# Score tiles of two key tiles, earlier transposes, and three loads in new places, in an attention and spectral-mixing kernel on one Trainium2 core

## The chip, the cores and the metric

The kernel runs on one core of one Trainium2 chip. The core has five engines with queues of their own: PE (TensorE: matrix products; its weight loads are listed as PEld), DVE (VectorE), ACT (ScalarE), POOL (GpSimd) and SP (SyncE, which here only issues DMA). An engine works through its own instructions in order and waits on semaphores for the others. Sixteen DMA engines move data between the chip's memory (HBM) and the on-chip SBUF; matrix products land in PSUM, of which this kernel uses eight banks.

The metric is the device time of one execution in microseconds. Three runs of the kernel before took 470.34, 473.37 and 477.15 us; the median is 473.37.

## The reference

Two layers follow each other. Sizes: batch B = 8, heads H = 8, sequence S = 576, head size D = 64, so the model width is 512; 64 Fourier modes.

```python
# attention: causal, window of 128, a linear bias per head
scores = matmul(q, k.T) / sqrt(64)
rel = pos[:, None] - pos[None, :]
bias = -slope[h] * abs(rel)                 # slope[h] = 2 ** (-8 (h + 1) / 8)
mask = (rel >= 0) & (rel < 128)
attn = softmax(where(mask, scores + bias, -1e9))
x = matmul(attn, v)                         # heads side by side: [8, 576, 512]

# spectral mixing
X = rfft(x, axis=1)[:, :64]
Yr = einsum('bmd,mde->bme', Xr, w_r) - einsum('bmd,mde->bme', Xi, w_i)
Yi = einsum('bmd,mde->bme', Xr, w_i) + einsum('bmd,mde->bme', Xi, w_r)
u = x + irfft(Y, n=576)
out = u + maximum(u @ w_ch, 0)
```

q, k and v have 28 MB together, w_r and w_i 67 MB each, w_ch 1 MB, the output 9.4 MB, all in float32.

## The kernel before, in words

**Units and slots.** A unit is a pair of heads s of one batch b; there are 32. Units of pair 0 come first (units 0 to 7), then pairs 1, 2 and 3 batch by batch (units 8 to 31). The main loop runs slots: slot n (`_slot`) does the scores of unit n, the transposes of unit n + 1, the casts of q and k of unit n + 2 and of v of unit n + 1, the product with v (`_av`) of unit n - 1 and the Fourier transform (`_spectrum`) of unit n - 2. The order in which the functions are called is the order of the instructions on each engine: nothing is rescheduled.

**One unit.** `_load_unit` loads q and k (rows of 2304 B on 128 partitions), `_load_v` the first 512 tokens of v (rows of 512 B). POOL casts them to bfloat16 (`_cast_qk`, `_cast_v`). PE transposes q and k in 36 small products (`_tr`, two PSUM banks), ACT evacuates them (`_evac`). `_score` makes one of four key tiles: eight (four pairs for two halves) products of 64x256 for two key tiles together, an exponential on ACT of 128x512 (448 for the last tile) and a product with a mask on DVE. The mask is exp(-slope x distance), zero outside the window, so the bias and the window cost one multiplication. `_av` multiplies by v with a column of ones, which gives the sum of the softmax beside the result, and DVE divides (L495 to L501). The PSUM tile `av` exists once, so the division of unit n - 1 has to be done before PE starts `av` of unit n.

**The last 64 tokens of v** of a head pair, for all batches, are one tile `vt` (`_load_vt`): two DMAs on POOL's own queue with runs of 256 B, cast on POOL (`_cast_vt`). For pair 0 that is done in the setup, for pairs 1 to 3 in slots 2 to 4 (loads) and 4 to 6 (casts).

**Weights of the modes.** The 512 input channels are split into group 0 (pair 0's 128 channels) and group 1 (the other 384). Group 0's weights are 32 tiles, each with two modes (2 x 512 KB), group 1's 64 tiles, one mode each (2 x 768 KB). `_modes` multiplies them; group 0 within slots 10 to 35, group 1 in the late stage. A ring of three tiles (RING = 3) holds them, so tile i + 3 is sent when PE has used tile i.

**SyncE's queue.** All loads but `vt` stand in one queue in the order written: the first 16 units before the loop, with the first three weight tiles among them, then in slot n unit n + 8, v of unit n + 5, and that slot's weight tiles. q and k have 9 buffers, v has 6. The program also makes each DMA of this queue wait for the one eight before it.

**The late stage.** After the slots, group 1's 64 tiles are loaded one after the other; between them PE does the channel products x @ w_ch (`_xt`, `_xw`), which need w_ch in bfloat16 (`g.wch`), and the inverse Fourier tables (`_ft`, into `g.FT`). w_ch is loaded in two halves in slots 12 and 16 and cast on POOL in slots 14 and 18. `_finish` then puts the output together.

**PSUM.** One bank for the modes (`acc`), two for `av`, one for the Fourier products (`xt`), two for scores (`sc`, 512 columns each, also used by `_spectrum_swap`), two for transposes.

## Time and profile before

| | |
|---|---|
| median of three runs | 473.37 us (470.34 to 477.15) |
| span of the profiled execution | 471.9 us; the page gives no other time of its own |
| PE / DVE / ACT / POOL busy | 359.0 / 230.7 / 190.2 / 157.5 us |
| mean granted clock of TensorE | 0.812 |
| moved by DMA | 174.00 MB, 369 GB/s over the span |
| waits of SyncE before group 1's weights | 94.1 us on PE's modes, 83.8 us on its transposes |
| PE's idle time before mode products of group 1 | 35.4 us, for wi |

How to read it: PE is busy most of the span, but much of that is waiting inside pipelined products and a lowered clock. The DMA share says how much of the time the sixteen DMA engines had packets; it comes out a little over 1 in places. The same share goes with different rates, since short rows cost more per byte. The attention's slots lie between about 8 and 173 us, group 0's last tiles are used at 185, the late stage runs to about 430, and the end (`_finish`) to 472.

### The profile page before, as it was taken

To read this page: it belongs to the slowest core of one execution; us is meant where nothing else is said; L and a number is where in the kernel's file an instruction comes from. 1 tells how busy PE (TensorE), PEld (TensorE's weight loads), DVE (VectorE), ACT (ScalarE), POOL (GpSimd) and SP (SyncE) were. 2 spreads that over 40 slices of the span, in tenths; PEclk is the share of its full clock that TensorE was granted. 3 is DMA by queue.
4 is the path that set the end of the run, shared out by engine and by line. 5 is a ranking of instruction groups with operands and counts; after the bars stand their busy time and mean duration, and the time that the engine had idled before them with its cause. 6 is when DMAs were issued, how large, how long until landed. Compare 5 with 4: busy or idle time off the path is not lost.

```text
span 471.9 us, 15044 instructions
## 1 busy us (share of the span) xinstructions
PE 359.0 (76%) x6417; PEld 240.8 (51%) x6417; DVE 230.7 (49%) x504; ACT 190.2 (40%) x359; POOL 157.5 (33%) x264
## 2 busy tenths in 40 slices
PE   2777687977988754789787788888878798746983
PEld 2655476766776642434444444444444465424542
DVE  8677866668586551342324333333333353103884
ACT  3887676576774720123211111111122132102772
POOL 7799975786784500001000000000000000000995
PEclk9988978596797995777978878777777789555998
DMA  8999989999999999998999999999999999992677
GB/s 247 352 360 291 306 264 380 389 394 391 365 372 367 341 350 419 423 422 331 355 409 421 424 422 424 422 421 420 423 422 423 422 411 420 422 425 109 251 269 269
DMA packets 60515, 174.00 MB, mean 369 GB/s; under 512 B 5920, under 2 KB 22304, under 8 KB 60448
## 3 DMA queue, kind: packets, MB, share of 16 engines
q1 hardware_dynamic: 60064, 171.99, 94.8%
q0 software_dynamic: 384, 1.05, 1.0%
q8 instruction: 50, 0.82, 0.7%
q14 instruction: 17, 0.14, 0.1%
HBM read 163.58 MB, written 9.44 MB: 367 GB/s over the span
## 4 chain that ended last, share of the span: by engine, by line
DMA 46%; PE 32%; DVE 7%; issue 7%; ACT 4%; POOL 2%; SPq 0%; POOLq 0%; ACTq 0%; DVEq 0%
DMA wi<-in_moe_w_i_dram 46%; PE sc L436 7%; PE tqk L410 4%; PE av L489 3%; PE xt L534 3%; PE xw L761 3%; PE acc L702 3%; PE acc L733 2%; PE acc L698 2%; PE mm L761 2%; ACT qkT L418 1%; PE tp L752 1%; DVE r L890 1%; ACT att L448 1%; POOL o L898 1%
## 5 line engine op out<-in xcount | busy, mean ns | idle before, releaser
L779 ACT CAST hl<-xw 128x512 bf16<-128x512 f32 x72 | 42.1, 585 | 153.3 <-PE xw L761 153.3
L898 POOL TENSOR_TENSOR o<-r,ys 128x512 f32<-128x512 f32 x25 | 30.8, 1279 | 214.6 <-ACT ys L889 214.6
L761 PE MATMUL xw<-wch,xT 128*64 128x512 bf16 x576 | 96.0, 474 | 0.0
L780 DVE TENSOR_TENSOR hl<-xw,hl 64x512 bf16<-64x512 f32 x72 | 50.0, 695 | 81.2 <-ACT hl L779 81.2
L448 ACT ACTIVATE att<-sc 128x512 bf16<-128x512 f32 (+1 forms) x128 | 73.0, 595 | 34.4 <-PE sc L436 33.0
L702 PE MATMUL acc<-Xlast,wi 128*128 128x16 bf16 x768 | 55.3, 193 | 35.4 <-DMA wi<-in_moe_w_i_dram 35.4
L399 POOL CAST vb<-v 64x256 bf16<-64x256 f32 x128 | 65.4, 511 | 20.0 <-PE av L489 14.4
L702 PEld LDWEIGHTS <-wi 128*128 128x128 bf16 x768 | 49.1, 103 | 39.2 <-DMA wi<-in_moe_w_i_dram 39.1
L698 PE MATMUL acc<-Xlast,wr 128*128 128x16 bf16 x768 | 58.8, 193 | 13.0 <-DMA wr<-in_moe_w_r_dram 10.3
L698 PEld LDWEIGHTS <-wr 128*128 128x128 bf16 x768 | 50.2, 103 | 35.7 <-issue 21.2
L451 DVE TENSOR_TENSOR att<-att,mask 128x512 bf16<-128x512 bf16 x96 | 51.5, 559 | 30.6 <-ACT att L448 30.3
L436 PE MATMUL sc<-qkT,qkT 64*64 64x256 bf16 (+1 forms) x512 | 52.0, 313 | 18.4 <-ACT att L448 5.8
L761 PEld LDWEIGHTS <-xT 128*64 128x64 bf16 x576 | 38.5, 134 | 40.3 <-issue 24.9
L436 PEld LDWEIGHTS <-qkT 64*64 64x64 bf16 x512 | 29.1, 121 | 27.8 <-issue 18.6
L418 ACT COPY qkT<-tqk 128x576 bf16<-128x576 bf16 x64 | 41.3, 647 | 4.3 <-PE tqk L410 4.3
L410 PE MATMUL tqk<-ident_b,qkb 64*64 64x64 bf16 x1152 | 32.0, 211 | 12.5 <-issue 7.2
L754 DVE COPY xT<-tp 128x512 bf16<-128x512 bf16 x36 | 15.2, 423 | 53.5 <-PE tp L752 53.0
L410 PEld LDWEIGHTS <-qkb 64*64 64x64 bf16 x1152 | 31.7, 127 | 12.8 <-issue 6.8
L489 PE MATMUL av<-vb,att 64*128 64x65 bf16 (+1 forms) x1024 | 30.1, 204 | 3.5 <-issue 3.5
L489 PEld LDWEIGHTS <-att 64*128 64x128 bf16 (+1 forms) x1088 | 25.1, 104 | 9.9 <-issue 6.7
L388 POOL CAST qkb<-k 128x576 bf16<-128x576 f32 x32 | 26.1, 815 | 0.7 <-PE tqk L410 0.7
L388 POOL CAST qkb<-q 128x576 bf16<-128x576 f32 x32 | 22.7, 711 | 6.1 <-PE tqk L410 3.9
(124 smaller groups left out, 480.8 us busy)
## 6 DMA issues: line engine op xcount, KB each, us to landing
wr<-in_moe_w_r_dram SPq DMA_DIRECT2D x64, 768.0 KB, 8.2
wi<-in_moe_w_i_dram SPq DMA_DIRECT2D x64, 768.0 KB, 9.6
wr<-in_moe_w_r_dram SPq DMA_DIRECT2D x32, 512.0 KB, 6.5
wi<-in_moe_w_i_dram SPq DMA_DIRECT2D x32, 512.0 KB, 7.0
q<-in_q_dram SPq DMA_DIRECT2D x32, 288.0 KB, 6.7
k<-in_k_dram SPq DMA_DIRECT2D x32, 288.0 KB, 6.3
v<-in_v_dram SPq DMA_DIRECT2D x64, 128.0 KB, 6.1
out_dram<-o SPq DMA_DIRECT2D x32, 256.0 KB, 2.2
```

Source lines behind the costliest of these rows:

```text
L388: g.nc.gpsimd.tensor_copy(tb, t)
L399: g.nc.gpsimd.tensor_copy(o[64 * hh : 64 * hh + 64, i], u.v[64 * i : 64 * i + 64, hh])
L410: g.nc.tensor.transpose(tp[hs, r, :], u.b[w][hs, r], g.ident_b[hs, hs], tile_position=(64 * hh, 64 * hh))
L418: g.nc.scalar.copy(dst.rearrange("c (p r) -> c p r", r=g.R), u.tp[w].rearrange("c r p -> c p r"))
L436: nc.tensor.matmul(sc[hs, r * nq : (r + 1) * nq], lhsT=kT[hs, kt * P + r : kt * P + P : 2], rhs=qT[hs, kt * P : kt * P + nq], start=True, ...
L448: nc.scalar.activation(a[:, :cols], sc[:, :cols], AF.Exp, scale=1.0 / math.sqrt(g.D))
L451: nc.vector.tensor_tensor(out=a, in0=a, in1=g.mask[:, s], op=ALU.mult)
L489: nc.tensor.matmul(av[o, hh, col(t)], lhsT=a[hs, c0 : c0 + m], rhs=vb[hs, 0 : D + 1], start=(j == 0), stop=(j == len(terms) - 1), tile_pos ...
L698: nc.tensor.matmul(o, lhsT=wr[:, a].bitcast(BF16)[:, 1::2][:, c], rhs=X[:, a, 1:3, :, m], start=(a == 0), stop=False)
L702: nc.tensor.matmul(o, lhsT=wi[:, a].bitcast(BF16)[:, 1::2][:, c], rhs=X[:, a, 0:2, :, m], start=False, stop=(a == A - 1))
L761: nc.tensor.matmul(out[64 * h : 64 * h + 64], lhsT=lhsT[h], rhs=rhs[h], tile_position=(0, 64 * h), **kw)
L780: nc.vector.tensor_tensor(out=hl[64:128], in0=xw[64:128], in1=hl[64:128], op=ALU.subtract)
```

## The change

- `_score` makes two key tiles in one PSUM tile of two banks (`sc`, one buffer, in the pool `ps2`), with one exponential of 1024 (or 960) columns and one mask product (`_masked`), where there were four of 512 and 448. Slot n does half 0, then half 1.
- Transposes run two units ahead (`n + 2`), k before q, one after each half of the scores; casts of q and k three units ahead. Evacuated q and k have three buffers instead of two. Slot 0 does units 1 and 2.
- `_spectrum_swap` uses the bank of `xt`.
- The last tokens of v go through SyncE's queue, after the loads of units 0, 10, 11 and 13, and DVE casts them, in the same slots as before.
- w_ch is loaded in one DMA after the slots, into the last four tiles of `hl` as a buffer, behind the first three tiles of group 1; POOL casts it in one operation. `FT` and `wch` are allocated in the late stage.
- In the setup the slopes are set by POOL, the distances of the last tile share a tile with the others, the first mask is made earlier and the others after slots 1, 2 and 3.

```diff
 def _score / _masked
+    sc = g.ps2.tile([P, 1024], FP32, tag="sc", name="sc")
+    for j in range(2):
+        c = 2 * k + j
+        nq = min(256, g.S - c * P)
...
+    a = g.work.tile([P, 1024], BF16, tag=f"att{k}", name=f"att{k}")
     nc.scalar.activation(a[:, :cols], sc[:, :cols], AF.Exp, scale=1.0 / math.sqrt(g.D))
...
+def _masked(g, n, k):
+    a, m = g.unit[n].att[k], g.mask[:, g.units[n][1]]
+    if k == 0:
+        a = a.rearrange("p (j c) -> p j c", j=2)
+        m = m[:, 0:512].unsqueeze(1).broadcast_to([P, 2, 512])
+    else:
+        a = a[:, 0:960]
+    g.nc.vector.tensor_tensor(out=a, in0=a, in1=m, op=ALU.mult)

 def _slot
+    nxt = [m for m in ((1, 2) if n == 0 else (n + 2,)) if m < N]
     if n < N:
         _score(g, n, 0)
-        _score(g, n, 1)
-    if n + 1 < N:
-        _tr(g, n + 1, 0)
-        _evac(g, n + 1, 0)
-        _tr(g, n + 1, 1)
+        _masked(g, n, 0)
+    for m in nxt:
+        _tr(g, m, 1)
+        _evac(g, m, 1)
     for w in w0:
         _modes(g, *w)
     if n < N:
-        _score(g, n, 2)
-    if n + 1 < N:
-        _evac(g, n + 1, 1)
-    if n < N:
-        _score(g, n, 3)
-    if n + 2 < N:
-        _cast_qk(g, n + 2)
+        _score(g, n, 1)
+    for m in nxt:
+        _tr(g, m, 0)
+        _evac(g, m, 0)
+    if n + 3 < N:
+        _cast_qk(g, n + 3)
     if n + 1 < N:
         _cast_v(g, n + 1)
+    if n < N:
+        _masked(g, n, 1)
...
-            if n == g.first[j + 1] - 6 + i:
-                _load_vt(g, s)

 _spectrum_swap
-    sw = g.ps1.tile([P, 4, 2, g.NM], FP32, tag="sc", name="sw")
+    sw = g.ps2.tile([P, 4, 2, g.NM], FP32, tag="xt", name="sw")

 _load_vt / _cast_vt, and where the first 16 units are loaded
-        g.nc.gpsimd.dma_start(
+        g.nc.sync.dma_start(
...
-    g.nc.gpsimd.tensor_copy(g.vbt[:, s, :, 0 : g.D], g.unit.pop(("vt", s)))
+    g.nc.vector.tensor_copy(g.vbt[:, s, :, 0 : g.D], g.unit.pop(("vt", s)))
...
+                    for i, s in enumerate(first):
+                        if n == (0, 10, 11, 13)[i]:
+                            _load_vt(g, s)

 the late stage
+            g.FT = zp.tile([P, 4, S], BF16)
+            g.wch = zp.tile([P, 4, DM], BF16)
...
+                _load_wch(g)
+                for t in line[ahead:]:
+                    _load_w(g, *t)
...
+def _load_wch(g):
+    t = g.hl[:, -4:].rearrange("p n h e -> p (n h e)").bitcast(FP32).rearrange(
+        "p (t e) -> p t e", t=4)
+    nc.sync.dma_start(out=t, in_=g.w_ch.rearrange("(t p) e -> p t e", p=P))
+    nc.gpsimd.tensor_copy(g.wch, t)
```

## The prediction

> **What bounds the kernel now.** I read the page's forty slices first, then the chain that ended last, then busy time by stretch, then the waits of the DMA queue, then the time line of single engines. The chain is 46% DMA for wi and the slices show 420 GB/s from slice 20 to 35. So the late stage is paid for in bytes. The change works on what comes before, so I cut the span by stage:

> ```profile
> 14.00:60.00 46.00, 32.99 (x848) 26.46 (x848) 35.53 (x89) 35.45 (x73) 42.62 (x74) 0.92 1.05 332
> 60.00:70.00 10.00, 8.95 (x252) 8.02 (x253) 5.97 (x18) 8.12 (x17) 7.67 (x13) 0.71 0.81 249
> 70.00:150.00 80.00, 66.30 (x1686) 55.00 (x1685) 54.69 (x133) 52.32 (x103) 56.64 (x97) 0.79 1.04 382
> 150.00:186.00 36.00, 24.15 (x633) 19.18 (x632) 16.77 (x48) 14.16 (x31) 8.30 (x18) 0.83 0.97 360
> 186.00:210.00 24.00, 17.94 (x210) 9.99 (x211) 7.54 (x13) 4.75 (x9) 0.17 (x2) 0.73 1.02 424
> 210.00:240.00 30.00, 22.90 (x305) 13.41 (x306) 9.70 (x23) 7.58 (x16) 1.98 (x12) 0.83 0.93 360
> 240.00:429.00 189.00, 150.21 (x2097) 87.78 (x2093) 60.04 (x98) 37.45 (x64) 0.00 (x0) 0.77 1.00 417
> ```
> Columns: stretch, length, busy time of PE, PEld, DVE, ACT, POOL with instruction counts, granted clock, DMA share, GB/s. From 14 to 150 us the DMA share is 1.04 to 1.05 except in one stretch, 60 to 70, where it falls to 0.81. The rate is lower before 60 (332 GB/s) than after 186 (424) at the same share, so the early bytes are dearer, not fewer: q and k rows are 2304 B, v rows 512 B, weight rows 4 to 6 KB.

> The hole at 60 has a cause on the SyncE queue and on PE:

> ```profile
> 33.43 1.03 SPq L364 DMA_DIRECT2D v<-in_v_dram  x2
> ...
> 46.21 0.89 SPq L364 DMA_DIRECT2D v<-in_v_dram  x2
> ...
> 59.67 0.89 SPq L364 DMA_DIRECT2D v<-in_v_dram  x2
> 62.87 0.56 SPq L650 DMA_DIRECT2D wr<-in_moe_w_r_dram  x1
> ```
> ```profile
> 41.04 0.41 PE L436 MATMUL sc<-qkT,qkT 64*64 64x256 bf16 x4 [2.42 <-ACT X L594]
> ...
> 60.73 0.63 PE L436 MATMUL sc<-qkT,qkT 64*64 64x256 bf16 x4 [2.42 <-ACT X L594]
> ```
> The fourth weight tile (62.87) may be sent only when PE has used the first, in slot 10, at 62.3. The queue has nothing else to send, and every later transfer stands behind it. So **the time at which PE reaches slot 10** is the first term of the end. After it, slots 10 to 23 each move 2.78 us of q, k and v (852 KB at the 306 GB/s of 47 to 59 us) and 0.9 weight tile of 1.05 MB at about 400 GB/s, 2.4 us: 5.1 us. Slots 24 to 33 with their tail move 19 tiles, about 50 us. That is 72 + 50 = 122 us from 62.9, and the last of these tiles is used at 185.2 (122.3 later). The middle is DMA-bound to within what this sum can resolve; what a faster slot could win there is the 0.97 and the dips of the shares above, at most 5 us.

> **The change, part by part.**

> *Scores in pairs.* Two exponentials of 597 ns (128x512) become one of 128x1024. The 448-column form is about 54 ns under the 512-column one, 0.84 ns a column, so one of 1024 is 597 + 430 = 1.03 us; a slot saves 2 x 0.16 us of ACT and, at 442 ns for a 512-column product, at most 0.2 us of DVE. Neither is on the path: ACT is busy 52 of 80 us, DVE 55. The price is the buffer: two score tiles of one bank become one tile of two banks. PE may write the second half-slot's scores only after the first exponential is through, and the next slot's only after the second. Eight score matmuls take 0.75 us and each exponential 1.03 plus about 0.2 of hand-over either way: 2 x (0.75 + 1.03 + 0.3) = 4.2 us is the least a slot can take. Early slots now end 3.5 to 5.5 us apart (their last exponentials end at 16.5, 20.2, 23.7, 29.2 with two masks in between, 32.9, 37.5), so before slot 10 this is a loss of 0 to 0.8 us a slot. From slot 10 on PE has 18 transposes (0.5 us) and 16 mode matmuls (0.55 us) to put under the 1.3 us of the first exponential, and more under the second: 0.25 us a slot is left open. Its bounds are nothing (DMA sets the slot) and 0.7 us (no mode tile in that half).

> *Transposes a unit further ahead, sw in the xt bank.* PE waits for evacuations (12.5 us in all for L418) and for the swap's bank (the two waits of 2.42 us above). Both go. The second stood right before slot 10, so 2.4 us come off there (in the 4.3 us a slot used below); the first falls under the stall below.

> *Setup.* The slopes go to POOL and three DVE operations on the distances merge; the mask is ready some 1.5 us sooner, but evacuations now stand behind it on ACT (2 x 0.65 us) and the first score behind those. I take nothing. Nor for the masks of three pairs after slots 1 to 3 (1.05 us of ACT each, as many as before), nor for FT, which nothing writes before the late stage.

> *Last tokens of v.* POOL loses eight issues (683 ns) and four casts (656 ns), 8 us, and its 4.2 us wait before the first cast: POOL is 93% busy from 14 to 60, so this is the largest relief of the change. But the casts now stand in DVE's queue, in slots 4, 5 and 6, **ahead of the division of the previous unit** (0.21 + 0.14 + 0.69 + 0.28 = 1.3 us), which frees PE's one av tile. And the transfers now stand in SyncE's queue behind loads 10, 11 and 13. Those loads are DMA-paced: load 10's v went out at 33.4, load 13's at 46.2 to 47.1. In the kernel before the same transfers went out past that queue, at slots 2 to 4, and the last was cast at 45.9. A transfer in SyncE's queue lands 6.1 to 6.7 us after issue, so the three land at about 41, 47 and 54, while slot 6 would come at about 42. DVE waits for the third until 54, casts (0.6), divides unit 5 (1.3), and PE does av of unit 6 at 56 to 57. Behind the waiting DVE stand the mask products and every division; behind those PE's av and slots 7 to 10. From 57 there are two whole slots of 4.3 us and the head of slot 10 (0.75 + 0.5 + 0.2): first mode matmul at 67.0 against 62.3. **+4.7 us.** Bounds: with slots of 3.5 us and a third landing at 52, 63.4 (+1); with no stall at all the hole at 60 closes (-2.4).

> What a 256-byte row costs in this queue no row shows. 852 KB at 306 GB/s with q and k at the weights' 424 leaves v 1.39 us for 512 packets on 16 engines, 43 ns each. The 4096 packets of the change then cost between the same time per byte (5.6 us) and the same per packet (11 us), against 4.7 us (1.0% of the span) in the software queue. It lies before 63 us, where SyncE will wait for PE anyway, so it counts only through the third landing: +0.7 to +4.7 us there; I take 0.7, by bytes, which is in the 54. [...]

> *w_ch late.* The two loads and two casts (1036 ns each) leave slots 12 and 16; 1 MB moves from one saturated stretch to another, 2.5 us each way, nothing. Its wait for freed memory is on the division of the last unit, at 173, before it can be issued at 186.3 behind tiles 1 and 2 of the last group; so it holds up nothing in the queue. But the first channel product now needs it. Before, PE does that product at 189.7 and tile 1 right behind it at 193. Now tiles 1 and 2 land at 192.2 and 195.9, w_ch at 198.4, its cast (2.07) ends at 200.7, the product takes 1.9, and tile 1 is released at 203.4 instead of 193.7. Tile 3, sent at 189.4, has landed by 202, so the DMA is empty for 2.5 to 3 us. Part comes back: two transfers then follow closely and the dip at 210 to 240 (360 GB/s, 4.5 us lost against 424), where PE's Fourier tables outlast the transfers in flight, starts with one more transfer in flight. **+1.5 us**, bounds 0 and +6.

> *Middle.* PE less tied to evacuations: **-1.0 us**, bounds -4 and +5 (22 slots x 0.25).

> **The sum.** 471.9 (span) + 4.7 + 1.5 - 1.0 = 477.1. The page gives the span alone; the three runs have a median of 473.37, 1.5 over it, which I take for what lies around the span. 477.1 + 1.5 = 478.6, say **478.5 us**, 1.1% over the median. A measurement of this kernel tells 2% from no change (463.9 and 482.8).

> **Rivals.**

> 1. *The single score tile sets every slot* (slower). Deciding point: the work PE has between the two halves of a slot against the 1.3 us of the exponential. If transposes are late (their casts on POOL now run one unit further ahead) or the modes wait for weights, 0.7 us a slot is open in 22 slots, 15 us: 478.5 + 15 = 493. For it: PE is at 83% of the stretch 70 to 150, so there is little slack to take it up. Against: DMA needs 5.1 us a slot there, 0.3 more than PE's 4.8. Chance 0.17.
> 2. *POOL's relief decides* (faster). If the transfers of v come early enough, slots 0 to 10 run without POOL's 93%, the hole at 60 closes (-2.4), and the middle wins its 4: 471.9 - 6.4 + 1.5 = 467. For it: POOL's casts, 815 and 511 ns on average against 657 and 391 at best, are the slowest part of an early slot. Against: the queue's times above. Chance 0.15.
> 3. *The change does nothing*: transfers set the middle and PE's lateness at slot 10 is made up, 473.4. For it: the 122 us that fit. Against: a transfer not sent at 63 is not sent later for nothing. Chance 0.13.

> My forecast has 0.55. Range: from 465 (rival 2 and a little) to 489 (the sum with the landing by packets, w_ch at +6 and the middle at +3); it leaves out most of rival 1 and the fast edge of rival 2. Faster by over 2%: 0.09, from rival 2. Slower by over 2%: 0.17 from rival 1 and 0.09 from the forecast's upper edge, 0.26. Within: 0.65.

> **What would show it.** In the profile after: DVE's casts of the last tokens wait for their DMA, the last until 53 to 57, and PE's av waits for the division behind it; the fourth weight tile goes out at 66 to 69; the stretch 60 to 70 has a DMA share under 0.8. POOL stands idle in 30 to 55 instead of 93% busy. PE waits for the cast of w_ch for about 11 us near 190 to 205 and the DMA share dips near 205. The share in 75 to 150 stays at 1.04. The prediction is wrong if the fourth weight tile goes out before 62, or if the slots from 10 on are over 0.5 us longer while the DMA share falls there.

## Result and the profile after

The changed kernel takes **491.33 us** (median of four runs, 487.79 to 495.16). The kernel before has a median of 471.89 us over four runs. Ratios, here and below, leave out executions more than 1.5% over the fastest of their kernel, so a ratio can differ from the quotient of two medians. The ratio is **1.0345**, with a 95% interval of 1.028 to 1.041: 16 us slower. The forecast was 478.5 us in a range of 465 to 489. The direction came true and the size did not, and neither did the likeliest class, within 2%.

The span of the profiled execution grew from 471.9 to 486.0 us, by 14.1. Busy time by stretch of the changed kernel, in the stretches of the prediction (columns: stretch, length, busy time of PE, PEld, DVE, ACT, POOL with counts, granted clock, DMA share, GB/s):

```profile
14.00:60.00 46.00, 29.50 (x750) 25.61 (x747) 23.33 (x54) 29.11 (x44) 29.61 (x52) 0.78 1.08 327
60.00:70.00 10.00, 5.85 (x185) 4.94 (x182) 7.62 (x18) 6.84 (x10) 7.59 (x15) 0.98 0.26 85
70.00:150.00 80.00, 63.48 (x1822) 56.40 (x1819) 49.99 (x109) 54.05 (x77) 54.20 (x96) 0.89 0.98 353
150.00:186.00 36.00, 24.43 (x654) 20.52 (x653) 18.54 (x43) 15.73 (x24) 9.85 (x21) 0.87 0.96 350
186.00:210.00 24.00, 7.07 (x97) 4.88 (x98) 1.67 (x4) 0.65 (x2) 2.49 (x5) 0.50 0.96 381
210.00:240.00 30.00, 25.90 (x361) 15.58 (x359) 12.73 (x27) 9.93 (x20) 1.98 (x12) 0.88 0.90 365
```

Two things stand out. The hole in the transfers from 60 to 70 us has grown: share 0.26 and 85 GB/s, where it was 0.81 and 249. And from 186 to 210 PE works 7.1 of 24 us at a granted clock of 0.50, where it worked 17.9 at 0.73. POOL has its relief (29.6 us busy from 14 to 60 instead of 42.6), and the kernel is slower all the same.

The hole, on SyncE's queue of the changed kernel, from the last load of v's last tokens (`vt`) on:

```profile
45.27 1.38 SPq L366 DMA_DIRECT2D vt<-in_v_dram  x2
...
61.02 0.89 SPq L357 DMA_DIRECT2D v<-in_v_dram  x2
72.10 0.58 SPq L647 DMA_DIRECT2D wr<-in_moe_w_r_dram  x1
```

After 61 the queue has nothing to send until PE has used the first weight tile in slot 10. The fourth one goes out at 72.10; before, it was 62.87. What PE waits for on the way there (start, duration, operation, in brackets the idle time before it and what ended it):

```profile
41.63 0.61 PE L564 MATMUL xt<-F,x_sb 128*128 128x128 bf16 x4 [3.65 <-DVE x_sb L499]
...
47.46 0.58 PE L576 MATMUL sw<-xn,swap 128*128 128x512 bf16 x1 [3.94 <-DVE x_sb L499]
...
50.62 0.96 PE L432 MATMUL sc<-qkT,qkT 64*64 64x256 bf16 x8 [1.10 <-ACT att L446]
...
61.27 0.57 PE L432 MATMUL sc<-qkT,qkT 64*64 64x256 bf16 x8 [0.66 <-ACT att L446]
...
69.50 0.38 PE L576 MATMUL sw<-xn,swap 128*128 128x512 bf16 x1 [2.66 <-DVE x_sb L499]
...
71.28 0.18 PE L729 MATMUL acc<-X,wr 128*128 128x32 bf16 x1 [0.56 <-ACT X L594]
```

There are three kinds of wait: one for the division that stands behind the casts of v's last tokens (41.63), one at each swap (47.46, which the second of these casts delays too, and 69.50), and a short one in every slot for the first exponential. At the swaps the row names the division, whose result the swap does not use. ACT's last reading of `xt`, the bank that the swap writes, ends at the same moment:

```profile
69.09 0.36 ACT L595 ACTIVATE X<-xt,par 128x128 bf16<-128x128 f32 x1
```

The second loss is in the late stage. SyncE and PE around w_ch (`hl` is the buffer it lands in):

```profile
193.76 0.39 SPq L671 DMA_DIRECT2D hl<-in_moe_w_ch_dram  x1
196.81 0.33 SPq L654 DMA_DIRECT2D wr<-in_moe_w_r_dram  x1
...
212.10 0.33 SPq L654 DMA_DIRECT2D wr<-in_moe_w_r_dram  x1
```
```profile
208.07 3.17 PE L757 MATMUL xw<-wch,xT 128*64 128x512 bf16 x16 [10.83 <-POOL wch L672]
```

PE stands 10.8 us before the first channel product, and no weight tile is sent for 15.3 us.

Where the 14.1 us of the span came from, read off SyncE's issues (tiles of group 1 counted from 1):

| stretch, between two issues or ends | before | after | difference | predicted |
|---|---|---|---|---|
| start to the fourth weight tile | 62.87 | 72.10 | +9.2 | +4.7 |
| to the first tile of group 1 | 116.8 | 115.5 | -1.3 | -3.5 (the middle's -1.0, and -2.5 for w_ch's megabyte) |
| to the 16th tile of group 1 | 59.1 | 64.7 | +5.6 | +4.0 (the hole's +1.5, and +2.5 for that megabyte) |
| to the last tile | 180.2 | 180.7 | +0.5 | 0 |
| to the end of the span | 52.9 | 53.0 | +0.1 | 0 |

The prediction let the megabyte's 2.5 us cancel; the table puts them where they were to fall. So the way to slot 10 was missed by 4.5 us, the middle by 2.2 and the start of the late stage by 1.6, each with its sign right. The runs below take this apart.

### The profile page after: what moved, and what is told of

It reads as the page before. It is cut to its first block, busy times and chain, and to the rows that moved or that the text cites. A ratio compares the mean times of both kernels' runs of the same rounds, so it can differ in the third digit from the quotient of the medians.

```text
span 486.0 us, 14808 instructions
## 1 busy us (share of the span) xinstructions
PE 348.0 (72%) x6417; PEld 240.2 (49%) x6417; DVE 216.8 (45%) x433; ACT 186.1 (38%) x295; POOL 146.5 (30%) x259
## 4 chain that ended last, share of the span: by engine, by line
DMA 52%; PE 27%; ACT 6%; issue 5%; DVE 4%; SPq 2%; POOL 1%; POOLq 0%; ACTq 0%; DVEq 0%
DMA wi<-in_moe_w_i_dram 44%; PE sc L432 6%; ACT att L446 5%; PE av L490 4%; DMA v<-in_v_dram 3%; PE xw L757 3%; PE acc L698 3%; DMA hl<-in_moe_w_ch_dram 3%; PE acc L694 2%; PE tqk L403 2%; PE mm L757 2%; PE xt L535 2%; PE tp L748 1%; DMA vt<-in_v_dram 1%; DVE r L886 1%
## 5 line engine op out<-in xcount | busy, mean ns | idle before, releaser
L757 PE MATMUL xw<-wch,xT 128*64 128x512 bf16 x576 | 91.9, 457 | 10.8 <-POOL wch L672 10.8
L446 ACT ACTIVATE att<-sc 128x1024 bf16<-128x1024 f32 x64 | 64.0, 1000 | 42.3 <-PE sc L432 33.6
L457 DVE TENSOR_TENSOR att<-att,mask 128x1024 bf16<-128x1024 bf16 x64 | 49.4, 773 | 50.8 <-ACT att L446 50.5
L432 PE MATMUL sc<-qkT,qkT 64*64 64x256 bf16 (+1 forms) x512 | 46.4, 298 | 26.8 <-ACT att L446 15.2
L392 POOL CAST vb<-v 64x256 bf16<-64x256 f32 x128 | 60.0, 469 | 17.2 <-PE av L490 11.6
L432 PEld LDWEIGHTS <-qkT 64*64 64x64 bf16 x512 | 32.1, 118 | 29.9 <-issue 20.4
L403 PE MATMUL tqk<-ident_b,qkb 64*64 64x64 bf16 x1152 | 35.9, 206 | 7.9 <-POOL qkb L381 4.9
L403 PEld LDWEIGHTS <-qkb 64*64 64x64 bf16 x1152 | 32.9, 122 | 10.6 <-POOL qkb L381 5.0
L750 DVE COPY xT<-tp 128x512 bf16<-128x512 bf16 x36 | 15.3, 424 | 49.2 <-PE tp L748 48.7
L381 POOL CAST qkb<-q 128x576 bf16<-128x576 f32 x32 | 24.7, 772 | 39.9 <-issue 27.5
```

Of the source, the lines that this page charges most:

```text
L381: g.nc.gpsimd.tensor_copy(tb, t)
L392: g.nc.gpsimd.tensor_copy(o[64 * hh : 64 * hh + 64, i], u.v[64 * i : 64 * i + 64, hh])
L403: g.nc.tensor.transpose(tp[hs, r, :], u.b[w][hs, r], g.ident_b[hs, hs], tile_position=(64 * hh, 64 * hh))
L432: nc.tensor.matmul(sc[hs, c0 : c0 + nq], lhsT=kT[hs, c * P + r : c * P + P : 2], rhs=qT[hs, c * P : c * P + nq], start=True, stop=True, ti ...
L446: nc.scalar.activation(a[:, :cols], sc[:, :cols], AF.Exp, scale=1.0 / math.sqrt(g.D))
L457: g.nc.vector.tensor_tensor(out=a, in0=a, in1=m, op=ALU.mult)
```

## The experiments

Ratios are to the kernel before, beside which each was run, with 95% intervals. "W4" is the time at which the fourth weight tile goes out. It is the measure of slot 10, and comes from the one profiled execution of each kernel.

### 1. v's last tokens back on POOL

```diff
 def _load_vt
-        g.nc.sync.dma_start(
+        g.nc.gpsimd.dma_start(
 def _cast_vt
-    g.nc.vector.tensor_copy(
+    g.nc.gpsimd.tensor_copy(
```
with the loads at the places of the kernel before (pair 0 in the setup, the others in slots 2 to 4).

> The changed kernel with the last tokens of v back in POOL's queue and cast by POOL. Theory (the casts wait in DVE's queue ahead of the divisions, which idles PE and drops its clock): the fourth weight tile goes out at 63 to 66 us instead of 72.1, the granted clock in 47 to 60 is back at 0.9 or more, and about 8 us go: 483 where the changed kernel has 491. Rival (the single score tile and the swap in the bank of xt make the early slots long): the fourth tile stays at 70 or later, and the time at 489 or more.

Measured: 491.68 us, ratio 1.0365 (1.031 to 1.042), W4 71.15. Nothing measurable is won. The stall has only changed its place, into the setup. On POOL and on PE of this run:

```profile
17.52 0.61 POOL L372 CAST vbt<-vt 128x512 bf16<-128x512 f32 x1 [5.24 <-DMA vt<-in_v_dram]
18.08 0.66 POOL L380 CAST qkb<-q 128x576 bf16<-128x576 f32 x1
```
```profile
19.40 0.69 PE L402 MATMUL tqk<-ident_b,qkb 64*64 64x64 bf16 x18 [4.14 <-POOL qkb L380]
```

In the changed kernel slot 0 transposes units 1 and 2, so PE needs the cast of unit 2 early. On POOL that cast stands behind the one of v's tokens, which waits for its DMA. The run therefore doesn't show that the casts in DVE's queue are harmless; it shows that this cast stalls somebody wherever it stands before its data has landed.

### 2. w_ch back in the slots

```diff
-                _load_wch(g)
...
+                    for i in range(2):
+                        if n == g.first[1] + 4 + 4 * i:
+                            _load_wch(g, i)
+                        if n == g.first[1] + 6 + 4 * i:
+                            _cast_wch(g, i)
```

> The changed kernel with w_ch loaded and cast in the slots, in two halves, as before. Theory (the first channel product waits for a late cast, so the ring of weight tiles runs dry): fourth tile at 72 as in the changed kernel, no gap of 15 us between tiles 3 and 4 of the last group, 2.5 us more for the megabyte in the middle and 5.7 less behind it, 3 to 6 us less in all, 486 to 488. Rival (the late stage is set by its bytes and would have lost the same in the Fourier tables): at most 1 us less.

Measured: 484.13 us, ratio 1.018 (1.0125 to 1.0235), W4 71.60. Late w_ch costs 1.65% of 474, about 8 us, with the error of two ratios in it (0.85% of the time). In the two traces the late stage is 6.1 us shorter in this run and the middle 4.1 us longer. The fourth and fifth tiles of group 1 go out at 200.86 and 205.00; the gap of 15 us is gone.

### 3. Both undone

The edits of runs 1 and 2 together. Of the change there remain the scores in pairs, the transposes further ahead, the swap in the xt bank and the setup.

> The changed kernel with both of these undone; what is left is the paired scores, the transposes two units ahead, the swap in the bank of xt and the setup. Theory (two stalls make the loss): 471 to 476, within 1% of the kernel before. Rival (the single score tile sets the slot, 0.25 to 0.7 us in each of 22): 480 to 487.

Measured: 485.64 us, ratio 1.0223 (1.017 to 1.027), W4 70.50. A stall in the setup is there as in run 1 (3.06 us), so this run doesn't take out the last tokens of v in full. But without those 3 us W4 would still be some 67.4, an estimate, 4.6 us late: the theory that v and w_ch were all of it falls. The swaps wait 2.71 and 2.96 us, and the second half of the scores waits 0.6 to 1.2 us in each slot.

### 4. The casts of v's last tokens three slots later

```diff
-                g.vts = actx.enter_context(tc.tile_pool(name="vts", bufs=2))
+                g.vts = actx.enter_context(tc.tile_pool(name="vts", bufs=3))
...
-            if n == g.first[j + 1] - 4 + i:
+            if n == g.first[j + 1] - 1 + i:
                 _cast_vt(g, s)
```

The loads stay where the change put them. The casts come in slots 7 to 9, when the data has long landed.

> The changed kernel with the casts of the last tokens of v three slots later (7 to 9 instead of 4 to 6), with a third buffer for them; their DMAs stay where the change put them, in SyncE's queue. Theory (only the place in DVE's queue hurts): PE has no wait over 3 us between 36 and 50, the fourth tile goes out at 63 to 67, about 483, as with the loads in POOL's queue. Rival (256-byte rows in SyncE's queue delay what stands behind them): the fourth tile at 69 or later, 487 or more.

Measured: 486.85 us, ratio 1.0242 (1.019 to 1.029), W4 67.84. No cast of these tokens waits any more. So the early casts were 4.3 us of slot 10's lateness and 1.0% of the time, about 5 us. That is close to the 4.7 us of the prediction for this one cause. The other 5 us of lateness are something else. PE at the second swap of this run, right before slot 10 (at the first one it waits 1.78 us):

```profile
65.03 0.59 PE L576 MATMUL sw<-xn,swap 128*128 128x512 bf16 x1 [3.96 <-DVE x_sb L499]
```

From this came a second theory: the lateness has three parts, the casts, the swaps in the xt bank and the single score tile. Run 5 takes out the swap's bank alone; runs 6 and 7 take the parts out one on top of the other.

### 5. The swap in the transposes' banks, all else as changed

```diff
 def _spectrum_swap
-    sw = g.ps2.tile([P, 4, 2, g.NM], FP32, tag="xt", name="sw")
+    sw = g.ps1.tile([P, 4, 2, g.NM], FP32, tag="tqk", name="sw")
```

> The changed kernel with the swap's tile in the transposes' two banks instead of the xt bank; all else is left. Theory: what makes slot 10 late has three parts, the last tokens of v (about 4 us), the two swaps that wait for the xt bank to be read out (1.5 to 4 us each, and the half clock that follows such a wait), and the single score tile (PE waits 0.7 to 1.2 us in each early slot for the first exponential). This run takes out the second part: the waits of 1.6 to 4 us on sw are gone, the fourth weight tile goes out at 66 to 69 instead of 72, and the time is 486 to 489 us. Rival: PE has no time to give in these slots, since the casts of v stand in DVE's queue and set slots 4 to 6; then the wait only turns into one on the transposes or on v, the fourth weight tile stays at 71 to 72 and the time at 490 to 492.

Measured: 495.88 us, ratio 1.0425 (1.033 to 1.052), W4 70.64. Slot 10 is 1.5 us earlier, where the theory had 3 to 6, and the time is no better (its interval overlaps that of the changed kernel). The rival is right in part: PE's wait for the division behind the first cast grew from 3.65 to 5.68 us. The swap still waits, for another thing:

```profile
46.85 0.61 PE L576 MATMUL sw<-xn,swap 128*128 128x512 bf16 x1 [2.67 <-DVE xn L569]
...
66.92 0.39 PE L576 MATMUL sw<-xn,swap 128*128 128x512 bf16 x1 [1.48 <-DVE xn L569]
```

The releaser is now `xn`, the copy of the spectrum that the swap multiplies. So the bank was not the whole of this wait, and the first mode product now waits 1.67 us for `X`, where it waited 0.56. W4 to the first tile of group 1 took 123.0 us in this execution, the longest of all (114 to 120 in the others). What lengthened it is open.

### 6. Casts late, swap in the transposes' banks, w_ch in the slots

The edits of runs 2, 4 and 5 together.

> The changed kernel with three parts taken out together: the last tokens of v are cast in slots 7 to 9, when they have landed (a third buffer), the swap stands in the transposes' banks, and w_ch is loaded and cast in the slots as before. What is left of the change are the scores in pairs, the transposes further ahead and the setup. Theory: v and the swap were 6 to 8 us of the lateness at slot 10 and w_ch 6; the fourth weight tile goes out at 62 to 65 and the time is 474 to 478 us. Rival: the single score tile holds PE in every slot and is the whole lateness; then the tile goes out at 68 to 71 and the time stays at 482 to 486, as in the run with both other parts undone.

Measured: 478.82 us, ratio 1.0104 (1.0045 to 1.016), W4 66.04. Between the two expectations for W4 and just over the theory's time. Against run 4 the swap's bank brings 1.8 us at slot 10. In the time the step from run 4 is 1.4%, and w_ch alone is worth 1.1 to 1.65% (runs 8 and 2), so nothing measurable is left for the swap in the time.

### 7. The same, with the product with v between the two halves of the scores

```diff
     for w in w0:
         _modes(g, *w)
+    if 0 <= n - 1 < N:
+        _av(g, n - 1)
     if n < N:
         _score(g, n, 1)
...
-    if 0 <= n - 1 < N:
-        _av(g, n - 1)
```

> The run before this one (v cast late, swap in the transposes' banks, w_ch in the slots) with one more edit: the product with v of unit n - 1 stands between the two halves of the scores of unit n, so that PE has more to do under the first exponential. Theory: the wait of 0.7 to 1.2 us a slot for that exponential goes in slots 1 to 9; the fourth weight tile goes out 3 to 5 us earlier than in the run without this edit, at 58 to 62, and the time is 470 to 475 us. Rival: the early slots are set by ACT and POOL and not by PE's wait, so the wait only moves to the second half or to the division; then the tile goes out within 1.5 us of the run without the edit, and the times are equal within 3 us.

Measured: 474.52 us, ratio 1.0029 (0.999 to 1.007), W4 64.04. That is 0.75%, or 3.5 us, better than run 6, though the two intervals touch, and no longer distinguishable from the kernel before. The profiled execution of this kernel took 479.4 us, 1% over its median, so only its early slots are read. There PE's waits for an exponential between 10 and 75 us fell from 10.2 to 4.3 us. Slot 10 comes 2.0 us earlier, between the theory's 3 to 5 and the rival's 1.5, while the time is the theory's. The price of the single score tile is what PE cannot do under the first exponential; the products with v fill more than half of that idle time, and a third of what they fill shows at slot 10.

### 8. w_ch late alone, in the kernel before

The edits of the change to w_ch and FT, and nothing else of it.

> The kernel before with one part of the change alone: w_ch is loaded in one DMA after the slots and cast in one operation on POOL, FT and w_ch in bfloat16 are allocated in the late stage. Theory: PE waits about 10 us for the cast with the products of tile 1 behind it, the fourth tile of group 1 goes out 10 to 18 us after the third, and the time is 3 to 7 us over the kernel before, 475 to 482. Rival: in the changed kernel w_ch only took up a lateness that was there already; alone it costs nothing, within 1.5 us of the kernel before, since the middle is shorter by the 2.5 us that its megabyte took there.

Measured: 479.13 us, ratio 1.0112 (1.005 to 1.017). PE waits 10.75 us for the cast, and the fifth tile of group 1 goes out at 206.28, 15.5 us after the fourth. This part alone costs 5.3 us; the rival, that it only took up a lateness that was there, falls. The middle is 2.0 us longer in this trace, not 2.5 shorter.

### 9. The channel products later, in the changed kernel

```diff
-                    while k < len(g.seq) and k * (NM - 10) < done * len(g.seq):
+                    while k < len(g.seq) and k * (NM - 10) < done * len(g.seq) and done >= 4:
```

> The changed kernel with one line more in the late stage: the channel products with w_ch begin only after the first four tiles of group 1, so that PE does not stand before the cast of w_ch with tiles 1 to 3 behind it; w_ch is loaded and cast as in the change. Theory: what the late w_ch costs is that wait (10.8 us) and the DMA that runs dry behind it; without it the fifth tile goes out at 198 to 204 instead of 212 and the time falls by 4 to 8 us against the changed kernel, to 483 to 487. Rival: the channel products only move into 210 to 240, where PE is the busiest engine, and the time comes back there: 489 to 491, with the last tile of group 1 sent at 431 or later.

Measured: 490.91 us, ratio 1.0348 (1.025 to 1.044): the same as the changed kernel. The wait of 10.8 us is gone and the fifth tile goes out at 202.37, as the theory said, and nothing measurable is won. SyncE, and busy time by stretch, of this run:

```profile
202.37 0.33 SPq L654 DMA_DIRECT2D wr<-in_moe_w_r_dram  x1
...
212.36 0.33 SPq L654 DMA_DIRECT2D wr<-in_moe_w_r_dram  x1
...
222.11 0.33 SPq L654 DMA_DIRECT2D wr<-in_moe_w_r_dram  x1
```
```profile
200.00:205.00 5.00, 1.10 (x24) 0.90 (x24) 0.00 (x0) 0.00 (x0) 0.00 (x0) 0.50 1.00 411
205.00:210.00 5.00, 1.10 (x24) 0.90 (x24) 0.00 (x0) 0.00 (x0) 2.09 (x3) 0.50 1.04 424
...
220.00:225.00 5.00, 4.83 (x62) 2.73 (x60) 2.89 (x5) 2.11 (x4) 0.00 (x0) 1.00 0.58 222
225.00:230.00 5.00, 2.89 (x57) 2.10 (x57) 2.07 (x9) 1.61 (x5) 1.21 (x8) 0.94 0.59 208
```

The hole in the transfers has moved from 205 to 215 (shares 0.75 and 0.37, 4.4 us without transfers) to 220 to 230 (0.58 and 0.59, 4.2 us). From 190 to 210 PE works 5.5 of 20 us in this run, 5.0 in the changed kernel and 16.2 in the kernel before. So taking the wait away does not take the cost away. While w_ch is under way PE has nothing to do but the short mode products. The channel products it owes come from 212.7 on, one after the other until 224.5, then the Fourier tables, and the weight tiles wait for both: the tile after the one of 222.11 goes out at 228.80. The rival is right.

### 10. v's last tokens alone, cast without a stall, in the kernel before

```diff
+                    if n in (0, 10, 11):
+                        _load_vt(g, max(0, n - 9))
...
+                    if n == g.first[1]:
+                        _load_vt(g, 3)
...
-        g.nc.gpsimd.dma_start(
+        g.nc.sync.dma_start(
...
-    g.nc.gpsimd.tensor_copy(g.vbt[:, s, :, 0 : g.D], g.unit.pop(("vt", s)))
+    (g.nc.vector if s else g.nc.gpsimd).tensor_copy(g.vbt[:, s, :, 0 : g.D], g.unit.pop(("vt", s)))
```
with the casts of pairs 1 to 3 behind the mask product of slots 7, 8 and 10; pair 0 is still cast on POOL.

> The kernel before with the last tokens of v alone moved, and cast without a stall: loads in SyncE's queue (behind units 0, 10 and 11, the third pair in slot 8), casts of pairs 1 to 3 on DVE at the end of slots 7, 8 and 10, when they have long landed. This is the relief of POOL (8 us of issues and casts) by itself. Theory: POOL does not set the early slots, the bytes of q, k and v do; the fourth weight tile goes out at 61 to 64 as before (62.9) and the time is within 2.5 us of the kernel before. Rival, the second one of the prediction: POOL's 93% was the limit; the tile goes out at 57 to 60 and the time is 465 to 469.

Measured: 473.82 us, ratio 1.0004 (0.9965 to 1.004), W4 63.15. The early stretch of this run:

```profile
14.00:60.00 46.00, 33.97 (x848) 27.08 (x845) 37.07 (x90) 35.17 (x71) 35.51 (x65) 0.84 1.04 321
```

POOL is 77% busy there instead of 93%, and slot 10 comes no earlier. POOL's relief brings nothing measurable in this kernel, and the new route of these transfers costs nothing measurable if nobody waits for them.

### 11. The swap one place later

Run 7 with the swap of the fourth and eighth unit in the next slot, behind the product with v (which now stands ahead of the mode products), and the casts of v's tokens behind the spectrum, at the end of their slots.

```diff
     if 0 <= n - 1 < N:
         _av(g, n - 1)
+    if 0 <= n - 3 < N:
+        j, s, b = g.units[n - 3]
+        if len(GROUPS[j]) == 1 and b % 4 == 3:
+            _spectrum_swap(g, j, b)
     for w in w0:
         _modes(g, *w)
```

> The kernel with pairs of scores, v cast late, w_ch in the slots, the swap in the transposes' banks and the product with v between the halves, with one more edit: the swap of the fourth and the eighth unit stands in the next slot, behind the first half of the scores, the transposes and the product with v, and the casts of the last tokens of v stand at the end of their slots. Theory: PE's waits of 1.2 and 2.9 us before the two swaps go, the fourth weight tile goes out at 60 to 62 instead of 64, and the time is 469 to 473, equal to the kernel before or 1 to 3 us under it. Rival: the transfers of q, k and v set slot 10 by then, or the first mode product still waits for the swap's result; the tile goes out at 63 or later and the time stays at 473 to 476.

Measured: 478.32 us, ratio 1.0076 (1.004 to 1.012), W4 66.87. Not faster than run 7; the intervals overlap, but slot 10 comes 2.8 us later. The swap itself no longer waits, but PE's waits before slot 10 have a new entry (waiting operation, releaser, us in total, times, longest):

```profile
PE acc L734 <- ACT X L598: 5.0, 1, 5.0
```

The first mode product of slot 10 needs the swap's result. Spectrum, copy `xn`, swap and four placements into `X` are a chain in front of it. The swap runs at 60.68, but DVE takes up its result only at 64.70, behind the next slot's mask product and division, so the chain ends later.

### 12. The same with w_ch late and the channel products later

Run 11 with the late w_ch of the change and the line of run 9.

> The kernel of the run before this one, but with w_ch loaded late as in the change and the channel products begun only after the first four tiles of group 1. Theory: its megabyte leaves the middle (2.5 us sooner at the first tile of group 1) and the late stage does not stand still, so it is 0 to 4 us faster than the run with w_ch in the slots: 467 to 472. Rival: the late cast or the channel products cost as much as the middle wins or more: 472 to 477.

Measured: 487.03 us, ratio 1.0159 (1.006 to 1.026), W4 65.75. By its ratio that is about 482 us at the 474.4 of the kernel before beside it: slower than either expectation. In the trace the middle is 3.6 us shorter than in run 11, as the theory wanted, and the start of the late stage 5.6 us longer.

None of the twelve is faster than the kernel before; runs 7 and 10 can't be told from it.

### What a late w_ch costs

Across all profiled executions but that of run 7, two stretches by where w_ch is loaded:

| w_ch | kernels | W4 to the first tile of group 1, mean (range) | first to 16th tile of group 1, mean (range) |
|---|---|---|---|
| in the slots | before, runs 2, 3, 6, 10, 11 | 118.1 us (116.8 to 119.6) | 58.8 us (56.0 to 60.2) |
| late | changed, runs 1, 4, 5, 8, 9, 12 | 118.3 us (114.1 to 123.0) | 64.6 us (63.6 to 65.8) |

The late stage pays 5.9 us more; the groups of the second column don't even overlap. The column before it mixes kernels that differ in more than w_ch. Four pairs differ in w_ch alone, the last one in the line of run 9 too. What late w_ch adds in each (us, and the difference of the ratios):

| in the slots; late | W4 to the first tile | first to 16th tile | time |
|---|---|---|---|
| before; run 8 | +2.0 | +4.5 | +1.1% |
| run 2; changed | -4.1 | +6.1 | +1.65% |
| run 3; run 1 | -0.3 | +4.8 | +1.4% |
| run 11; run 12 | -3.6 | +5.6 | +0.8% |

The late stage pays 5.3 us in the mean of these pairs. What the middle gives back scatters from -4.1 to +2.0, -1.5 in the mean of single traces. In time the four cost 5.9 us in the mean, with an error of about 2 us from the ratios' intervals. That is nearer to nothing given back (5.3) than to the full 2.5 us (2.8), but no proof of it. How much of its 2.5 us the megabyte gives back in the middle stays open.

There is no sign either that a kernel that reaches slot 10 late makes it up: of the thirteen kernels of the first table the six with W4 over 70 need 119.0 us to the first tile in the mean, the seven with W4 under 68 need 117.6.

### The sum by parts

From the changed kernel towards the one before, in ratios: the early casts 1.0% (run 4), w_ch and the swap's bank together 1.4% (run 4 to run 6), the empty time under the first exponential 0.75% (run 6 to run 7), the rest 0.3% (run 7, from nothing to 0.7%). Each step carries an error of half a per cent or more. At slot 10 the same steps are 4.3, 1.8 (the swap), 2.0 and 1.2 us of the 9.2.

## Why the prediction was wrong

**Right.** The place of the first bound and its mechanism: the fourth weight tile waits for slot 10, and the transfers for it. The landings of v's tokens were forecast for 41, 47 and 54 us and came some 1 to 2 us sooner; DVE in the changed kernel:

```profile
39.88 0.64 DVE L373 CAST vbt<-vt 128x512 bf16<-128x512 f32 x1 [5.04 <-DMA vt<-in_v_dram]
...
44.74 0.49 DVE L373 CAST vbt<-vt 128x512 bf16<-128x512 f32 x1 [1.55 <-DMA vt<-in_v_dram]
...
53.33 0.88 DVE L373 CAST vbt<-vt 128x512 bf16<-128x512 f32 x1
```

The third cast did not wait for its data; it stood behind a DVE that was late already. The cost put on the early casts, 4.7 us, is what run 4 gives for them, 4.3. The exponential of 1024 columns was put at 1.03 us and takes 1.02. The 0.25 us a slot left open from slot 10 on is 5.9 us of PE's waits in all, 0.27 a slot over 22 slots, and the DMA share from 75 to 150 us stays at 1.03, so it was hidden, as the sum took it. PE's wait for w_ch (10.8 us for about 11) and the release of tile 1, put at 203.4 without the lateness, fit: 8 us later it is 211.4, and the next tile went out at 212.1.

**The price of a 256-byte row.** The trace of the changed kernel has every packet of these transfers. The 4096 packets of 256 B took 26 ns each in the mean (median 19), those of v with 512 B took 29 (median 27). So the price is nearly the same per packet, 0.10 against 0.057 ns a byte, and the choice "by bytes" was wrong in kind. It was right in size by luck, because a 512-byte packet takes 29 ns and not the 43 of the prediction: 4096 packets of 26 ns on 16 engines are 6.7 us, near the 5.6 by bytes and far from the 11. The third landing, by 53.3, shows none of the 4 us that the upper price would have added.

**First step that failed: "Both go. The second stood right before slot 10, so 2.4 us come off there."** The swap's two waits were put down to the score bank it shared. The runs show a chain instead: last spectrum product, `xn`, swap, `X`, first mode product. The bank only decides at which link PE stands: before the scores in the kernel before (2.42 us), before the swap for `xt` to be read out in the changed one (2.66), for `xn` in run 6 (2.39), before the first mode product in run 11 (5.0). So the 2.4 us were not there to come off. Run 4 shows how much hangs on this: none of its casts waits, and W4 is 67.84, 5.0 us later than in the kernel before, where the prediction had "with no stall at all the hole at 60 closes (-2.4)". The swap's bank (1.8 us), the empty time under the first exponential (2.0) and 1.2 us of unknown cause make up these 5.0. (The 12.5 us of waits for evacuations in the same sentence count PE's weight loads, 7.0, with its products, 5.4.)

**Second step: "PE does av of unit 6 at 56 to 57 ... From 57 there are two whole slots of 4.3 us".** PE was taken at full clock. After the stalls its granted clock is half of that:

```profile
38.00:40.00 2.00, 0.00 (x0) 0.00 (x0) 0.12 (x1) 1.23 (x2) 1.76 (x5) 0.99 1.10 269
40.00:42.00 2.00, 0.37 (x4) 0.34 (x4) 1.88 (x6) 0.00 (x0) 1.05 (x2) 0.50 1.26 196
...
52.00:54.00 2.00, 2.00 (x48) 1.67 (x45) 1.33 (x2) 1.16 (x2) 1.77 (x3) 0.50 1.06 338
54.00:56.00 2.00, 1.31 (x28) 1.17 (x24) 1.54 (x6) 1.10 (x2) 1.66 (x4) 0.50 0.96 309
56.00:58.00 2.00, 2.00 (x35) 1.74 (x36) 0.65 (x1) 1.43 (x3) 0.41 (x1) 0.50 1.09 358
58.00:60.00 2.00, 2.00 (x49) 1.90 (x49) 1.38 (x4) 0.52 (x1) 1.94 (x4) 0.50 1.06 348
60.00:62.00 2.00, 1.34 (x48) 1.25 (x43) 1.17 (x3) 1.65 (x3) 0.88 (x3) 0.89 0.79 274
```

(These are stretches of 2 us of the changed kernel, columns as above; the granted clock is the third number from the end.) Run 4, which has no such stall, has half clock too, from 37.2 to 54.2, and PE's longest wait in the 3.41 us before that was 0.83 us. The scores of slots 6 to 9 begin at 47.98, 53.6, 58.95 and 63.0: slots 6 and 7 take 5.6 and 5.4 us at half clock, slot 8, in which the clock returns, takes 4.1. So it was not the third cast that held up slot 8, but PE itself, and slot 8 began 2.0 us later than the 57 of the prediction. From there the account closes: slots 8 and 9 take 4.1 and 3.8 us, 0.7 less than the two of 4.3; the swap's wait with its product adds 3.0; the head of slot 10 is 1.5 us as predicted. 2.0 - 0.7 + 3.0 = 4.3 us, and the first mode product came at 71.3 instead of 67.0. The single score tile is a part of every one of these slots: filling the time under the first exponential brought 2.0 us over ten slots (run 7), inside the 0 to 0.8 us a slot that the prediction gave.

**Third step: "1 MB moves from one saturated stretch to another, 2.5 us each way, nothing."** The bytes came in the late stage and came off the middle in part at most. Busy time from the first to the 16th tile of group 1, in the kernel before and in the changed one:

```profile
179.64:238.76 59.12, 41.60 (x543) 24.28 (x544) 17.23 (x36) 12.91 (x26) 2.63 (x16) 0.76 0.97 391
187.61:252.31 64.70, 38.48 (x543) 23.93 (x544) 17.22 (x36) 12.92 (x26) 4.46 (x17) 0.74 0.94 377
```

That is 23.1 MB at 391 GB/s and 24.4 MB at 377. Of the 5.6 us some 3.3 are the 1.3 MB more, at 391 GB/s, and 2.3 the lower rate. The hole was put at 2.5 to 3 us and is 4.4. But part of it does come back, as the prediction said: the dips of the kernel before from 210 to 235 (shares 0.74, 1.02, 0.86, 0.95 and 0.98, together some 2.3 us) are gone in the changed kernel, whose share from 215 to 240 is 1.00 or more. So the net price of the hole, 2.3 us, is near the 1.5. What failed is the "nothing" for the megabyte: the middle is 1.3 us shorter, where 1.0 and 2.5 were to come off, and the pairs above leave open what it gave back. Alone, a late w_ch costs 5.3 us (run 8), close to the bound of +6.

**A smaller one: "Setup. I take nothing."** The first exponential begins at 14.8 us instead of 13.5. The first six slots then take as long as before. Run 7 keeps this and ends 1.2 us late at slot 10; that the setup is the cause was not tried.

**The rivals.** The first, "the single score tile sets every slot", has its price right in kind and its place wrong: not the 22 slots of the middle, where DMA covers it, but the ten before. The second, POOL's relief, is refuted by run 10. The third, that a lateness is made up, by the time and the stretches above. Slower by over 2% had 0.26 and deserved more: the bound of +6 for w_ch was nearer to the truth than its +1.5, and the swap's chain and the half clock had no cost at all in the sum.

## What to carry to other kernels

When a change makes an engine wait, price the work behind the wait and not only the wait: PE worked at half clock for 20 us behind these stalls (39.97 to 60.45), and work that it owed came due with other work. A wait that names a bank may be one link of a chain; before taking it off, ask which link is next (spectrum, copy, swap, placement here). And don't let the bytes of a moved transfer cancel: a megabyte cost its full price where it went, and what it gave back where it came from was less sure, 1.5 us in the mean of four pairs that scatter by 6.

## What was unexpected of the hardware

In the traces of the kernel before and of the changed one the granted clock is 1.00 or 0.50 (a stretch across a change shows a mean), and the points at which it changes, 47 in the one and 45 in the other, lie whole multiples of 3.41 us apart. In the changed kernel it falls at 39.97, 2.0 us into PE's idle time, and comes back at 60.45, six times 3.41 us later. The 3.41 us up to 60.45 are the first of the six in which PE works without a break; the two before hold 0.4 and 0.7 us of idle time, and work without a break from 50.62 to 55.28 did not bring the clock back. The stretch up to 39.97 holds 0.9 us of PE's work. In run 4 the fall came without a long idle time: the clock falls at 37.17, after a stretch with 1.8 us of work and no idle time over 0.83.
